# Preparing the next slab of a chunked recurrence over four steps instead of two, with masks on ScalarE and GpSimd and all scalings on GpSimd

## The chip, the cores and the metric

The kernel runs on one core of one Trainium2 chip. The metric is the device time of one execution in microseconds (us); lower is better. TensorE (PE in the rows; its weight loads are PEld), VectorE (DVE), ScalarE (ACT), GpSimd (POOL) and SyncE (SP, which here only issues DMAs) each run their own instruction stream in program order; they meet through semaphores.

## What is computed

Three stages in a row: a linear recurrence with a state of 40 x 40 for each of 32 (batch, head) pairs over 768 positions, a mixture-of-experts layer with one expert per token, and a dense feed-forward layer with squared ReLU. The change touches the first alone:

```python
for t in range(S):                               # S = 768, D = 40, B*H = 32
    kt, vt, rt = (k[:, :, t], v[:, :, t], r[:, :, t])
    wt, at, bt = (w[:, :, t], a[:, :, t], b[:, :, t])
    y[:, :, t] = np.einsum('bhd,bhde->bhe', rt, state)
    Sa = np.einsum('bhde,bhe->bhd', state, at)
    state_decay = state * wt[:, :, None, :] - np.einsum('bhd,bhe->bhde', Sa, bt)
    state = state_decay + np.einsum('bhd,bhe->bhde', vt, kt)
...
x = _moe_ref(x=x, **moe_kwargs)
return _moe2_ref(x=x, **moe2_kwargs)
```

## The kernel before

**Tiling.** The 768 positions are cut into 24 chunks of 32. Inside a chunk the recurrence becomes matrix products over all 32 heads, and one chunk is one step of the loop in `run` (c = 0 to 23). Four chunks are a slab; r = c % 4 is a step's place in its slab.

**One step** is a list of stages in the order of ORD: Z0 Z1 (the state against the chunk's operands, L214), Y0 Y1 (output of the chunk before, L259, brought to the tile xt by VectorE in steps r=0 and 1, and by ScalarE and GpSimd in r=2 and 3), U0 U1 (Ust, L231, which reads the inverse in tile tt), V0 V1, T0 T1 (transposes of the state, L250, copied to ys by ScalarE), K0 K1 (KBt, transposes of kb, L205, copied to ys by ScalarE), R (RUV, L141 with the tile ym, masked by VectorE at L143) and S0 S1 (Sst, the new state: L241 on TensorE, then tile m by VectorE at L244). Z0 of the next step waits for m. x_part (L405) brings finished outputs to the next stage of the network.

**Preparation of later slabs.** While a slab is worked on, the chunks of the slab after the next are prepared:
- `decay` (L108 to L112), once for each pair of chunks: four scans and two reciprocals on VectorE, from the loaded w; its last piece loads the w of a later pair.
- `prod` (L121, L124), once per chunk: a is scaled by pp, and the two halves of kb by qq. A string such as 'VGG' says which engine takes each of the three: V is VectorE, G is GpSimd.
- `L` (64 matmuls of `heads`, L141 with a, kb): the chunk's triangular matrix in PSUM, masked by VectorE into tile zs (L143), stored to DRAM (nt), loaded back in another layout (`tul`, tile tu), and `post`, two copies on ScalarE (L128, L129) and two small products on VectorE (dl).
- `inv` (L169 to L173): the inverse of all 128 triangular matrices of a slab in place in tu, 113 small operations on VectorE in one chain, then a store to DRAM (td); `ttfill` brings it from there into tile tt for Ust, a quarter per step.

**What sets the order.** The order is written out by hand. A step has 33 positions; stage k moves on by PW[k] of them (Z0 is position 0, Y0 2, U0 6, T1 14, K0 16, R 18, S0 20, S1 23), and what `sched` holds at a position is issued there, in program order on its engine. The tables, with d the step counted from the beginning of the slab two before the one that is prepared (so d=4 is the first step of the slab just before it):
- CA=(1, 2, 20): the first decay at d=1, over positions 2 to 20; CB=(3, 0, 20): the second at d=3, over 0 to 20.
- PA: for each of the four chunks d, position and engines of prod.
- LP: for each of the four chunks d and the stage behind which its L stands.
- IB=(0, 4, 6, 99): how much of the inverse (in estimated us) is issued in steps r=0 to 3; in r=1 from position 8 on, in r=3 over positions 0 to 14.

Slab 0 uses IB0 for the inverse of slab 1; chunks 0 to 7 are prepared ahead of the loop or in step 0. All loads and stores of this part are on SP's queue, in program order, among them kb (K1 of a step loads the chunk that stands 8 later) and the fill of tt.

In the rows, L141 with `a,kb` is L, with `r,ut` RUV.

## Time and profile before

| | us |
|---|---|
| median of three runs | 1075.1 (1071.02 to 1076.72) |
| the profiled execution | 1071.28 |
| its span, first to last instruction | 1069.5 |
| TensorE busy | 875.9 (82% of the span) |
| VectorE busy | 685.0 (64%) |
| ScalarE busy | 437.6 (41%) |
| GpSimd busy | 330.9 (31%) |

The shares are means over two very different parts: the recurrence up to about 530 us, and the feed-forward layers after it, where TensorE is nearly always busy. What a change in the recurrence is worth is read from its steps. A step here begins with the first matmul of Z0; step 4 begins at 149.2 us, step 20 at 460.9. "PEclk" in a table of stretches is TensorE's granted clock as a share of the full 2.4 GHz, so 0.50 is 1.2 GHz for the whole stretch. A wait is put down to what ended last before it; "issue" means that nothing in the profile shows what was waited for.

### The profile page before, as it was taken

The page shows a single profiled execution, that of the slowest core. Times are in us where ns is not written, and L with a number is a line of the kernel's source. Part 1 is how long each engine was busy: PE and PEld are TensorE (multiplying, and loading weights), DVE is VectorE, ACT ScalarE, POOL GpSimd, SP SyncE. Part 2 cuts the span into 40 slices and gives each one's busy share as a digit, 9 for nine tenths or more (in the row PEclk, how much of TensorE's full clock was granted, in tenths as well). Part 3 has the DMA queues.
Part 4 walks back from the last instruction along what each step waited for, and adds up shares of the span by engine and source line. Part 5 has one row for each costly group of instructions (what it writes and reads, how often), then busy time and mean ns, then how long its engine had stood idle before and what let it go on. Part 6 is the DMA issues. An engine that isn't in the chain of part 4 may idle for free.

```text
span 1069.5 us, 32862 instructions
## 1 busy us (share of the span) xinstructions
PE 875.9 (82%) x14040; PEld 836.1 (78%) x14040; DVE 685.0 (64%) x1621; ACT 437.6 (41%) x872; POOL 330.9 (31%) x292
## 2 busy tenths in 40 slices
PE   1137679888878877778769988889999999999996
PEld 1136668777767767767659888889999999999996
DVE  7997678867776878873559898555344444444331
ACT  6233245444434344445356445334333333344331
POOL 6032422611622526736443223261111111100000
PEclk9997576766766878897669999989999999999999
DMA  7547757457455547478469887711100111100000
GB/s 185 127 108 235 184 144 175 123 140 169 120 139 145 124 106 179 133 197 222 134 188 284 281 274 240 221 57 32 30 15 26 29 31 32 31 27 13 14 14 16
DMA packets 128144, 132.22 MB, mean 124 GB/s; under 512 B 80201, under 2 KB 104559, under 8 KB 127987
## 3 DMA queue, kind: packets, MB, share of 16 engines
q1 hardware_dynamic: 123731, 118.95, 41.0%
q0 software_dynamic: 4256, 11.06, 3.4%
q8 instruction: 112, 1.84, 0.7%
q14 instruction: 45, 0.37, 0.1%
HBM read 104.79 MB, written 29.70 MB: 126 GB/s over the span
## 4 chain that ended last, share of the span: by engine, by line
PE 56%; DVE 22%; DMA 10%; issue 6%; ACT 2%; POOL 1%; SPq 0%; DVEq 0%; POOLq 0%; ACTq 0%
PE fps L554 20%; PE fps L561 17%; PE pr L141 4%; PE ps L231 3%; PE pr L259 3%; DVE tu L170 2%; DVE m L244 2%; DVE tmp L169 2%; PE ps L220 2%; DVE qq L108 2%; PE ps L405 2%; DVE ym L143 2%; PE ps L250 2%; DVE zs L143 1%; PE ps L241 1%
## 5 line engine op out<-in xcount | busy, mean ns | idle before, releaser
L554 PE MATMUL fps<-xl,w1h 128*128 128x256 f32 x768 | 198.8, 286 | 12.7 <-DVE xl L544 12.7
L554 PE MATMUL fps<-xh,w1h 128*128 128x256 f32 x768 | 199.7, 287 | 2.8 <-ACT xh L543 2.2
L554 PEld LDWEIGHTS fps<-xl,w1h 128*128 128x128 f32 x768 | 149.0, 194 | 14.7 <-DVE xl L544 14.6
L561 PE MATMUL fps<-w2h,hh 128*128 128x320 f32 x512 | 158.7, 310 | 0.0
L561 PE MATMUL fps<-w2h,hl 128*128 128x320 f32 x512 | 158.2, 309 | 0.0
L561 PE MATMUL fps<-w2l,hh 128*128 128x320 f32 x512 | 158.2, 309 | 0.0
L554 PEld LDWEIGHTS fps<-xh,w1h 128*128 128x128 f32 x768 | 148.7, 194 | 4.1 <-ACT xh L543 3.1
L662 DVE TENSOR_TENSOR g<-r 128x512 f32<-128x512 f32 x96 | 68.2, 711 | 81.1 <-ACT r L661 81.1
L664 DVE TENSOR_TENSOR hl<-g,hh 128x512 fp32r<-128x512 f32 x96 | 76.0, 792 | 66.0 <-ACT hh L663 66.0
L554 PE MATMUL fps<-xh,w1l 128*128 128x256 f32 x512 | 103.9, 285 | 0.0
L663 ACT CAST hh<-g 128x512 fp32r<-128x512 f32 x96 | 59.6, 621 | 94.8 <-DVE g L662 94.8
L561 PEld LDWEIGHTS fps<-w2l,hh 128*128 128x128 f32 x512 | 96.1, 188 | 0.0
L561 PEld LDWEIGHTS fps<-w2h,hh 128*128 128x128 f32 x512 | 96.1, 188 | 0.0
L561 PEld LDWEIGHTS fps<-w2h,hl 128*128 128x128 f32 x512 | 96.1, 188 | 0.0
L124 POOL TENSOR_TENSOR kb<-kb,qq 104x512 f32<-104x512 f32 x48 | 63.9, 1354 | 87.2 <-DVE qq L108 25.8
L661 ACT ACTIVATE r<-fps 128x512 f32<-128x512 f32 x96 | 57.1, 594 | 76.6 <-PE fps L554 76.6
L141 PE MATMUL pr<-a,kb 40*64 40x32 f32 x1536 | 39.6, 265 | 51.9 <-POOL kb L124 29.3
L554 PEld LDWEIGHTS fps<-xh,w1l 128*128 128x128 f32 x512 | 80.4, 194 | 0.0
L141 PEld LDWEIGHTS pr<-a,kb 40*64 40x64 f32 x1536 | 36.7, 188 | 54.2 <-POOL kb L124 29.5
L170 DVE TENSOR_TENSOR tu<-tu,tmp 128x120 f32<-128x120 f32 (+25 forms) x312 | 76.7, 287 | 0.1
L259 PE MATMUL pr<-ym,ys 128*40 128x32 f32 x1536 | 49.6, 227 | 32.6 <-DVE xt L262 14.2
L169 DVE TENSOR_TENSOR tmp<-tu 128x120 f32<-128x120 f32 (+25 forms) x312 | 73.1, 272 | 0.5
(142 smaller groups left out, 1709.7 us busy)
## 6 DMA issues: line engine op xcount, KB each, us to landing
kb<-in_kb SPq DMA_DIRECT2D x24, 416.0 KB
ut<-in_vE SPq DMA_DIRECT2D x24, 416.0 KB
raw<-in_w SPq DMA_DIRECT2D x16, 512.0 KB
raw<-in_w SPq DMA_DIRECT2D x16, 480.0 KB
w<-in_w SPq DMA_DIRECT2D x12, 468.0 KB
a<-in_a SPq DMA_DIRECT2D x24, 208.0 KB
r<-in_r SPq DMA_DIRECT2D x24, 208.0 KB
c<-in_w_out SPq DMA_DIRECT2D x7, 640.0 KB
```

The costliest lines, as they stand in the source:

```text
L124: e[1+j].tensor_tensor(out=kv,in0=kv,in1=q[:,:,:,1:17],op=ALU.mult)
L141: nc.tensor.matmul(pt[64*hf:64*hf+64,r,32*p:32*p+32],w[k,8*hf+p,:],x[k,8*hf+p,:],start=True,stop=True)
L143: nc.vector.tensor_tensor(out=out[64:128,16*hf:16*hf+16].rearrange('p (x r) t -> p x r t',r=2), in0=pt[64*hf:64*hf+64,:,0:256].rearrange(' ...
L169: if k==0: V.tensor_tensor(out=tv,in0=Tv[:,j:j+1,b0:b0+n].to_broadcast([128,j,n]),in1=Tv[:,0:j,j:j+1].to_broadcast([128,j,n]),op=ALU.mult)
L170: else: V.tensor_tensor(out=w,in0=w,in1=tv,op=ALU.add)
L259: nc.tensor.matmul(pt[64*par:64*par+40,32*(k//2):32*(k//2)+32],ys[:,h,:],ym[:,h,:],start=True,stop=True)
L554: nc.tensor.matmul(pt[:,256*u:256*u+256],a,b,start=i==0,stop=i==len(ops)-1)
L561: nc.tensor.matmul(pt[:,0:320],a,b,start=first and n==0,stop=last and n==23); n+=1
L661: nc.scalar.activation(out=r,in_=v,func=AF.Relu)
L662: V.tensor_tensor(out=g,in0=r,in1=r,op=ALU.mult)
L663: nc.scalar.copy(out=gh[:,2*m2:2*m2+2],in_=g)
L664: V.tensor_tensor(out=gl[:,2*m2:2*m2+2],in0=g,in1=gh[:,2*m2:2*m2+2],op=ALU.subtract)
```

## The change

For all slabs but the first two:
- the first decay moves from d=1 (positions 2 to 20) to d=0 (positions 5 to 15); the second stays at d=3, over positions 0 to 8;
- prod of the four chunks goes to d=1, 2, 3 and 4 (before: 2, 2, 3 and 4), all three scalings on GpSimd;
- L stands behind S1 of d=1, 2 and 3, and behind T1 of d=4 (before: U1 and S1 of d=3, U1 and T1 of d=4);
- of the inverse, 8 instead of 4 estimated us are issued in r=1.

Chunks 8 to 11 (P == 2) have tables of their own, nearer to the old ones. For every chunk from 8 on, the mask of L is replaced: ScalarE copies from PSUM to zs with a factor of +1 or -1 per partition (the new tile sgn), and GpSimd sets the triangle above to zero with two affine_select instructions of 32 x 1024.

```diff
-    IB=(0, 4, 6, 99)
+    IB=(0, 8, 6, 99)
...
-    CA=(1, 2, 20)
-    PA=((2, 11, 'VGG'), (2, 12, 'GGG'), (3, 21, 'VGG'), (4, 2, 'VGG'))
-    CB=(3, 0, 20)
+    CA=(0, 5, 15)
+    CA2=(1, 2, 20)
+    PA=((1, 4, 'GGG'), (2, 2, 'GGG'), (3, 9, 'GGG'), (4, 0, 'GGG'))
...
+    CB=(3, 0, 8)
...
-    LP=((3, 'U1'), (3, 'S1'), (4, 'U1'), (4, 'T1'))
+    LP=((1, 'S1'), (2, 'S1'), (3, 'S1'), (4, 'T1'))
...
+        s.sgn=T('sgn',[128,1]); G.memset(s.sgn,1.0); G.memset(s.sgn[96:128],-1.0)
...
-    def heads(s,w,x,out,mask):
+    def heads(s,w,x,out,mask,later=False):
...
+        if later:
+            for hf in range(2):
+                nc.scalar.activation(out=out[64:128,16*hf:16*hf+16].rearrange('p (x r) t -> p x r t',r=2),
+                    in_=pt[64*hf:64*hf+64,:,0:256].rearrange('p r (x t) -> p x r t',t=32),func=AF.Copy,scale=s.sgn[64:128])
+            for b in (96,64):
+                nc.gpsimd.affine_select(out=out[b:b+32],in_=out[b:b+32],pattern=[[0,32],[1,32]],compare_op=ALU.is_ge,fill=0.0,base=-1,channel_multiplier=-1)
+            return
...
-        s.heads(kb,a,zs,s.mask[64:128,0])
+        s.heads(kb,a,zs,s.mask[64:128,0],c>7)
```

What stands on VectorE at the end of step 11 (r=3 of slab 2), before: the end of the inverse (L169 to L171, tile tu), the mask of L at U1 (L143, zs) among it, the second decay (L108, L112), then ym and m.

```order
L169 TENSOR_TENSOR tmp<-tu 128x52
L143 TENSOR_TENSOR zs_109<-pr,mask 64x512 x2
L132 TENSOR_TENSOR dl_132<-pp_100,qq_105 40x16
L133 TENSOR_TENSOR dl_132<-pp_100,qq_105 40x16
L112 RECIPROCAL inv<-pp_102 104x32
L170 TENSOR_TENSOR tu<-tu,tmp 128x26x3
L170 TENSOR_TENSOR tu<-tu,tmp 128x26x2
L169 TENSOR_TENSOR tmp<-tu 128x54 x2
L170 TENSOR_TENSOR tu<-tu,tmp 128x27x2 x2
L171 SCALAR_TENSOR_TENSOR tu<-tu 128x28 x3
L171 SCALAR_TENSOR_TENSOR tu<-tu 128x29
L108 SCALAR_TENSOR_TENSOR pp_102<-w_86,inv 104x576
```

The same place after (lines of the changed kernel: L112 and L116 are the decay, L180 to L182 the inverse):

```order
L116 RECIPROCAL inv<-pp_102 104x32
L181 TENSOR_TENSOR tu<-tu,tmp 128x25x3
L180 TENSOR_TENSOR tmp<-tu 128x78
L112 SCALAR_TENSOR_TENSOR pp_102<-w_86,inv 104x576
L180 TENSOR_TENSOR tmp<-tu 128x52
L112 SCALAR_TENSOR_TENSOR qq_106<-w_86,inv 104x576
L181 TENSOR_TENSOR tu<-tu,tmp 128x26x3
L181 TENSOR_TENSOR tu<-tu,tmp 128x26x2
L180 TENSOR_TENSOR tmp<-tu 128x54 x2
L181 TENSOR_TENSOR tu<-tu,tmp 128x27x2 x2
L182 SCALAR_TENSOR_TENSOR tu<-tu 128x28 x3
L182 SCALAR_TENSOR_TENSOR tu<-tu 128x29 x2
```

The mask and its dl products are gone from here, the decay's last scan (qq) has come ahead of the inverse's last operations, and only 23 of the inverse's 113 instructions are left in this step, where 47 stood; r=1 now has 55 instead of 32, r=2 35 instead of 34.

GpSimd from step 9 (r=1) into step 10 (r=2), before: the scatters of the finished slab (L428), the copy of xr, both halves of xt, then kb and a of the two chunks that are prepared.

```order
L450 COPY gt_200<-xr_196 128x4
L428 DMA xs<-xr_196,slot 2048x388 x4
L409 COPY xr_196<-xr_196 128x64
L262 TENSOR_TENSOR xt<-xt,pp_103 104x256 x2
L124 TENSOR_TENSOR kb_91<-kb_91,qq_105 104x16x32 x2
L121 TENSOR_TENSOR a_88<-a_88,pp_101 104x512
L124 TENSOR_TENSOR kb_92<-kb_92,qq_105 104x16x32 x2
```

After, with the first select of zs_109 waiting for the landing of the three later scatters:

```order
L440 DMA xs<-xr_199,slot 2048x388
L125 TENSOR_TENSOR a_87<-a_87,pp_101 104x512
L128 TENSOR_TENSOR kb_91<-kb_91,qq_105 104x16x32 x2
L440 DMA xs<-xr_199,slot 2048x388 x3
L421 COPY xr_199<-xr_199 128x64
L151 AFFINE_SELECT zs_109<-zs_109 32x1024 x2
L273 TENSOR_TENSOR xt<-xt,pp_103 104x256
L125 TENSOR_TENSOR a_88<-a_88,pp_101 104x512
L128 TENSOR_TENSOR kb_92<-kb_92,qq_105 104x16x32 x2
L273 TENSOR_TENSOR xt<-xt,pp_103 104x256
```

The first chunk's scalings have come a step earlier, in among the scatters; the second chunk's stand between the two halves of xt; the selects are new.

SP's queue in step 11, before: the store of the inverse (td), then the loads of w, kb, r and ut, then the fill of tt.

```order
L183 DMA td<-tu 128x1024
L97 DMA w_86<-in_w 104x1152
L101 DMA kb_94<-in_kb 104x1024
L197 DMA r<-in_r 104x512
L197 DMA ut<-in_vE 104x1024
L190 DMA tt<-td 32x8x32 x4
```

After:

```order
L101 DMA w_86<-in_w 104x1152
L194 DMA td<-tu 128x1024
L105 DMA kb_94<-in_kb 104x1024
L208 DMA r<-in_r 104x512
L208 DMA ut<-in_vE 104x1024
L201 DMA tt<-td 32x8x32 x4
```

The load of w has come ahead of the store.

## Rows read from the trace of the kernel before

**Rows 1.** Table of stretches, steps 7 to 16 and 20; columns named in its first line.

```profile
core 0: us, PE busy (x) PEld busy (x) DVE busy (x) ACT busy (x) POOL busy (x), PEclk, DMA share, GB/s
205.00:226.60 21.60, 19.02 (x496) 17.20 (x496) 21.20 (x67) 9.34 (x23) 8.26 (x6) 0.68 0.42 112
226.60:252.50 25.90, 21.20 (x512) 19.55 (x505) 11.39 (x31) 10.18 (x24) 2.58 (x3) 0.60 0.63 153
252.50:269.60 17.10, 13.12 (x369) 11.79 (x368) 16.44 (x64) 6.17 (x16) 5.03 (x5) 0.80 0.87 203
269.60:286.80 17.20, 14.81 (x369) 13.48 (x368) 10.45 (x42) 7.56 (x19) 12.18 (x8) 0.70 0.49 114
286.80:307.10 20.30, 15.68 (x497) 14.16 (x496) 19.96 (x65) 10.24 (x24) 8.71 (x6) 0.82 0.38 102
307.10:333.10 26.00, 22.92 (x509) 20.97 (x504) 12.58 (x33) 9.52 (x22) 3.04 (x3) 0.50 0.72 170
333.10:352.20 19.10, 14.90 (x369) 13.64 (x368) 15.35 (x61) 6.39 (x16) 6.35 (x5) 0.71 0.54 137
352.20:366.70 14.50, 11.35 (x369) 9.80 (x368) 12.91 (x42) 7.78 (x20) 11.68 (x8) 1.00 0.57 140
366.70:388.00 21.30, 16.60 (x500) 15.01 (x502) 20.93 (x66) 9.93 (x23) 8.42 (x7) 0.77 0.29 77
388.00:411.90 23.90, 18.31 (x506) 16.83 (x504) 17.01 (x34) 10.20 (x23) 10.51 (x9) 0.64 0.57 134
460.90:474.20 13.30, 11.78 (x373) 10.40 (x372) 7.79 (x20) 7.94 (x20) 5.36 (x5) 1.00 0.72 193
```

**Rows 2.** Chain of waits, 300 to 316 us: start, length, what.

```profile
302.56 4.67 DMA td<-tu
...
307.30 6.90 DMA tt<-td
```

**Rows 3.** TensorE in order of time, step 8: start, length, instruction.

```profile
234.00 2.49 PE L231 MATMUL ps<-z,tt 64*32 64x40 f32 x64
```

**Rows 4.** Table of stretches, VectorE's instructions on tile tu alone, step 11.

```profile
286.80:307.10 20.30, 8.98 (x46) 0.82 0.38 102
```

**Rows 5.** Groups of instructions by shape: total busy us, mean ns of one, idle before.

```profile
L143 DVE TENSOR_TENSOR zs<-pr,mask 64x512 f32<-64x512 f32 x48 | 33.1, 689 | 26.5 <-PE pr L141 25.8
...
L121 DVE TENSOR_TENSOR a<-a,pp 104x512 f32<-104x512 f32 x18 | 15.5, 868 | 0.1
...
L121 POOL TENSOR_TENSOR a<-a,pp 104x512 f32<-104x512 f32 x6 | 8.0, 1328 | 14.1 <-DVE pp L108 14.1
...
L661 ACT ACTIVATE r<-fps 128x512 f32<-128x512 f32 x96 | 57.1, 594 | 76.6 <-PE fps L554 76.6
```

**Rows 6.** Line 108 (the decay's scans): durations in ns, min/median/max.

```profile
L108 DVE TENSOR_TENSOR_SCAN pp<-w,one x12: 1331/1350/2282, 7.0 to 371.7; 104x576 f32<-104x576 f32 x12
```

**Rows 7.** GpSimd in order of time, steps 10 and 17.

```profile
271.83 6.16 POOL L262 TENSOR_TENSOR xt<-xt,pp 104x256 f32<-104x256 f32 x2 [1.39 <-ACT xt L261]
...
421.14 1.59 POOL L727 TENSOR_TENSOR c64t<-c64t,c 128x640 int32<-128x640 int32 x1
```

**Rows 8.** VectorE in order of time, step 17, beside the second row above.

```profile
420.87 2.79 DVE L170 TENSOR_TENSOR tu<-tu,tmp 128x65 f32<-128x65 f32 x2
```

**Rows 9.** TensorE in order of time: L of one chunk in steps 11 and 12.

```profile
291.94 1.14 PE L141 MATMUL pr<-a,kb 40*64 40x32 f32 x64
...
316.92 1.93 PE L141 MATMUL pr<-a,kb 40*64 40x32 f32 x64
```

**Rows 10.** GpSimd's groups at the start: its selects, mean ns of one.

```profile
L70 POOL TENSOR_SCALAR_AFFINE_SELECT mask<-mask 32x64 f32<-32x64 f32 x2 | 0.5, 240 | 0.1
...
L379 POOL TENSOR_SCALAR_AFFINE_SELECT us<-us 128x128 f32<-128x128 f32 x1 | 0.3, 292 | 0.1
```

**Rows 11.** SP's queue in order of time: when the loads of kb were issued.

```profile
304.57 0.33 SPq L101 DMA_DIRECT2D kb<-in_kb  x1
...
330.30 0.49 SPq L101 DMA_DIRECT2D kb<-in_kb  x1
```

**Rows 12.** GpSimd in order of time, step 12: the scaling that waited for kb.

```profile
310.70 2.80 POOL L124 TENSOR_TENSOR kb<-kb,qq 104x512 f32<-104x512 f32 x2 [3.75 <-DMA kb<-in_kb]
```

More of the change, by code (lines that the diff above doesn't have):

```diff
@@ L28 @@
     F3=0
-    CA=(1, 2, 20)
-    PA=((2, 11, 'VGG'), (2, 12, 'GGG'), (3, 21, 'VGG'), (4, 2, 'VGG'))
-    CB=(3, 0, 20)
+    CA=(0, 5, 15)
+    CA2=(1, 2, 20)
+    PA=((1, 4, 'GGG'), (2, 2, 'GGG'), (3, 9, 'GGG'), (4, 0, 'GGG'))
+    PA2=((2, 2, 'GGG'), (2, 8, 'GGG'), (3, 9, 'GGG'), (4, 0, 'GGG'))
+    CB=(3, 0, 8)
     SC=(2, 14)
     L0=('R', 'S1')
-    LP=((3, 'U1'), (3, 'S1'), (4, 'U1'), (4, 'T1'))
+    LP=((1, 'S1'), (2, 'S1'), (3, 'S1'), (4, 'T1'))
+    LP2=((2, 'S1'), (3, 'U1'), (3, 'S1'), (4, 'T1'))
     YP=(0, 0, 1, 1)
@@ L312, in run @@
                 if P>=s.NS or P<2: continue
-                if d==4: at(0,*[lambda x=x: s.tul(x) for x,(e,st) in zip(range(2*A,2*A+4),s.LP) if e<4])
-                if d==s.CA[0]: add(s.decay(A),*s.CA[1:])
+                CA,PA,LP=(s.CA2,s.PA2,s.LP2) if P==2 else (s.CA,s.PA,s.LP)
+                if d==4: at(0,*[lambda x=x: s.tul(x) for x,(e,st) in zip(range(2*A,2*A+4),LP) if e<4])
+                if d==CA[0]: add(s.decay(A),*CA[1:])
                 for k in range(4):
-                    e,p,w=s.PA[k]
+                    e,p,w=PA[k]
                     if d==e: at(p,lambda x=2*A+k,w=w: s.prod(x,eng(w)))
-                    e,st=s.LP[k]
+                    e,st=LP[k]
                     if d==e: Ls.setdefault(st,[]).append(2*A+k)
```

## The prediction

> **What bounds the kernel now.** I read the table of stretches first, one row per step, then the chain of waits at a slab's border, then who holds which engine there. The feed-forward part (from 530 us on) is not touched, so everything is decided in the scan, steps 1 to 19. Its steps differ by position r in the slab. The last rows of the table hold the yardstick: step 20, with no preparation left, takes 13.3 us at a granted clock of 1.00 [rows 1]. Against it r=3 takes 21.6, 20.3 and 21.3, and VectorE is busy for 21.20, 19.96 and 20.93 of that: VectorE bounds r=3. r=1 is bounded by it as well (16.44 busy of 17.1; 15.35 of 19.1). r=0 takes 25.9, 26.0 and 23.9 with VectorE at only 11.39, 12.58 and 17.01: there TensorE is busy 21 to 23 us at clocks of 0.60 and 0.50, so the matmuls run mostly at the lower of the two levels (1.2 GHz) after a step in which TensorE had waited. r=2 is the cheapest, 17.2 at clock 0.70 and 14.5 at clock 1.00 [rows 1].
>
> Between r=3 and r=0 lies a chain: the last column of the inverse on VectorE, the store td (302.56, 4.67 us), the fill tt (307.30, 6.90 us), ending at 314.20 [rows 2], on which Ust of r=0 waits. From the start of r=3 (286.8) that is 27.4 us; one slab earlier Ust began at 234.00 [rows 3], 29.0 after 205.0. Mean 28.2. A shorter r=3 is worth only what this chain gives.
>
> **The change, part by part, for one full slab** (three of them: the pairs of steps 7-8, 11-12 and 15-16).
>
> (1) *From r=3 to Ust of r=0.* In r=3, 24 of the 47 operations of the inverse are gone (23 go to r=1, one to r=2). 46 of them took 8.98 us [rows 4], 0.195 each: -4.7. The mask of the chunk that stood at U1 goes from VectorE: two instructions of 0.689 [rows 5], -1.4, and it stood ahead of the inverse's end. The second decay is squeezed into positions 0 to 8, so its fourth scan, which stood behind the inverse, now stands ahead: +1.35 [rows 6]. The end of the inverse was 15.8 after the step's start (302.56 less 286.8 [rows 1, 2]), and comes to 11.0. But the three scalings of the third chunk are now on GpSimd in the same stretch, and they need the scans just ahead of the last columns. Two operations of the two engines that both read two SBUF operands don't run together: a GpSimd operation of 1.59 us beside a pair of inverse operations that lasted 2.79 [rows 7, 8] instead of the 0.4 that 0.195 each gives; and a pair of GpSimd operations of 256 elements that took 6.16 us under VectorE's back-to-back work [rows 7], where one of 512 takes 1.33 [rows 5]. So either VectorE stands for 3 x 1.33 = 4.0, and the inverse ends at 15.0, or GpSimd waits and it ends at 11.0. I take the middle, 13.0. From there to tt it was 11.65 (302.56 to 314.20 [rows 2]). The w load that stood between td and the fill now stands ahead of td; the fill can gain from nothing to the 2.2 that bring its 6.90 down to td's 4.67; I take 1. Ust starts at 13.0 + 10.65 = 23.6 instead of 28.2: **-4.6**, bounds -7.8 and -1.5. Late next is tt itself: r=3 ends earlier than it lands, so part of what VectorE is relieved of only lengthens the wait in r=0.
>
> (2) *From Ust of r=0 to r=1.* This took 18.5 (234.0 to 252.5) and 18.9 (314.2 to 333.1) [rows 1 to 3]. Two chunks' L stood in it, now one: -1.93 at the lower level [rows 9]. Its two masks run on ScalarE, ahead of the ys copies that Sst waits for: two of about 0.594, the nearest row for 512 elements from PSUM [rows 5], 0 to +1.2; TensorE has KBt and RUV between, which hide it at the lower clock. **-1.5**, bounds -1.9 and -0.7. The first decay, now here, takes 5.4 of VectorE's idle time. The nt store, which the tul, the next kb and ut loads stand behind on SP, waits for GpSimd's first select instead of VectorE's mask. Selects of 64 and 128 elements took 0.240 and 0.292 [rows 10], so 1024 take about 1.0 by that slope. Store and kb load go 1.2 later (0.59 x 2 and 1.0 against 1.4, rounded up for the handover).
>
> (3) *r=1.* VectorE loses four scans (5.4) and gains 23 operations of the inverse (4.5): 15.9 busy comes to 15.0. The scalings of the first chunk can stop it for up to 4.0. So 15 to 19 against lengths of 17.1 and 19.1: **0**, bounds -2 and +2. The kb load was issued at 304.57 [rows 11] and GpSimd got its data at 310.70 [rows 12], 6.1 later; the load for this step was issued at 330.30, so its data come at 336.4, or 337.6 with the delay of (2), 4.5 into r=1. Three scatters and the copy of xr are queued behind that wait on GpSimd, and the step's selects wait for the scatters to land, with the nt store behind them on SP; the loads that follow there (v, ra, tt, kb) have most of a step of slack.
>
> (4) *r=2.* A chunk's L now stands behind S1: 1.14 at the higher level, 1.93 at the lower [rows 9], part of it in the wait for m. Behind it on ScalarE stand z and the xt copies of the next step, up to 1.2 later each. **+1.2**, bounds -0.5 and +3. Scalings of a cost GpSimd 1.33 where VectorE took 0.868 [rows 5].
>
> The sgn memsets lie in GpSimd's idle start and cost nothing; without that cover they would be two memsets at the start.
>
> **The sum.** -4.6 - 1.5 + 0 + 1.2 = -4.9 a slab, -14.7 for three. Slab 0 is prepared by the old table with the new masks and scalings: half, -2.5. In slab 4 the inverse alone moves from step 19 to step 17: 4.5 us go over, between -4.5 and +4.5, taken as 0. Together -17. The profiled execution took 1071.3 (span 1069.5, 1.8 around it), so 1054; the median of the three runs is 1075.1, 3.8 above that execution, and I put the forecast on it: **1058**. Bounds by the terms: three slabs between -12.2 and +2.8 each, so 1075 less 37 and plus 8, with the ends 1031 to 1088.
>
> **The rivals.**
> *The clock stays up (B).* If r=3 no longer leaves TensorE waiting, r=0 runs at 2.4 GHz. The same L took 1.93 and 1.14 [rows 9], a ratio of 0.59; 18.7 us behind Ust come to 11.0, 7.7 less for each of three slabs, -23 on top: 1035. For it: step 14 at 1.00 took 14.5 [rows 1]. Against it: the wait for tt in r=0 stays, and grows.
> *Nothing is left (C).* VectorE stands still for all of GpSimd's scalings: (1) -1.5, (2) -0.7, (3) +2, (4) +1: 0.8 a slab, +2 in all, 1077. For it: the 2.79 us pair [rows 8].
> *GpSimd becomes the bound (D), slower.* In r=2 its queue is: half of xt, three scalings, the other half of xt, as the rows of the order show. If each group waits as the pair of [rows 7] does (6.16 less 1.33 for the same 512 elements: 4.8), it takes 6.16 + 4.8 + 4.0 = 15.0; it starts some 2.2 into the step (271.83 less 269.6), so x_part and L behind S1 get their data at 17.2, and with L and x_part the step ends at about 19.5 against 15.9: +3.6. TensorE waits for that, and the next step runs at the lower clock, 17.2 against 14.5 for a step of the same work [rows 1]: +2.7. With (1) -1.5, (2) -0.7 and (3) +2 that is +6.1 a slab, +18: 1094. It decides from the point where GpSimd's data for L come later than S1, some 13 us into the step. For it: the 6.16; against it: VectorE has less to do in r=2 (10.45 and 12.91 busy [rows 1]), so GpSimd should wait in one group, not two.
>
> The Trainium skill speaks against this change: "GPSIMD Engine Reference", section "Engine selection", gives elementwise work with two inputs to VectorE, as GpSimd takes about twice as long, and its "Key points" say that it shares SBUF interfaces with VectorE and collides with VectorE instructions that read two SBUF operands. The trace agrees with both (1.33 against 0.868, and the 2.79 us pair). By that rule alone the time would be that of C or D.
>
> **Chances.** A (forecast) 0.48; B 0.19; C 0.16; D 0.17. About 0.5% (5 us) is what a measurement of this kernel can tell from no change. Faster: A and B, 0.67. Same: C, 0.16. Slower: D, 0.17. The range leaves out the lower third of B and the upper part of D: 1031 to 1086.
>
> **What would show it.** r=3 at 16 to 19 us with VectorE still busiest; td issued 11 to 15 us into r=3 and Ust of r=0 some 23.6 after r=3's start; r=0 at 20 to 24; r=1 within 2 of 18; r=2 one longer. L behind S1 should not wait for kb. Wrong would be: r=2 or r=1 at 19 and more with TensorE waiting for kb or xt (D); pairs of inverse operations over 2 us in all steps (C); r=0 at a clock near 1.00 (B).

## The result, and the profile after

The changed kernel is slower: 1085.1 us (median) against 1073.5 us of the kernel before on the same chip, a ratio of 1.0121 (95% interval 1.0077 to 1.0165). On a second chip it was 1083.9 against 1073.3, 1.0094 (1.0058 to 1.0129). So it costs 10 to 13 us, where a gain of 17 was forecast. The 1085.1 us still lie inside the stated range (1031 to 1086), at its slow end; the direction was wrong. The profile taken with the first times fell on a disturbed execution (1925 us, with TensorE's matmuls at about twice their usual time), so the profile after is that of the run e1_after below, an execution of 1083.6 us.

> The changed kernel as it is, for a profile of an undisturbed execution. Expected 1.012 of the kernel before, some 1087 us, since that is what its times gave. By the forecast's own steps r=3 should be 16 to 19 us long, Ust of r=0 come 23.6 us after the start of r=3, r=0 take 20 to 24, r=1 17 to 19, r=2 one more than before. Theory D (GpSimd is the bound): r=2 or r=1 at 19 us and more, TensorE waiting there for what GpSimd makes. Theory C (VectorE stands still for GpSimd): pairs of operations of the inverse over 2 us in all four steps and r=3 no shorter than 20. Theory M (the masks on ScalarE and GpSimd): waits of TensorE for z and xt copies, 1 to 3 us in each step with an L behind S1. The step that is longer than before names the one to follow.

The table of stretches of the changed kernel, in the columns of [rows 1]: steps 3, 5 to 17, and last the whole scan from step 0 to the end of step 22.

```profile
133.10:154.60 21.50, 16.88 (x500) 15.31 (x496) 21.25 (x43) 12.42 (x27) 11.85 (x10) 0.76 0.39 100
...
177.30:196.00 18.70, 17.55 (x435) 16.11 (x434) 16.84 (x78) 6.80 (x17) 8.49 (x9) 0.59 0.73 183
196.00:212.60 16.60, 14.75 (x436) 13.17 (x432) 16.32 (x45) 9.93 (x23) 8.01 (x8) 0.79 0.49 123
212.60:232.90 20.30, 15.48 (x440) 13.88 (x432) 19.96 (x40) 9.93 (x23) 11.63 (x8) 0.77 0.36 97
232.90:254.70 21.80, 15.27 (x440) 13.72 (x436) 12.04 (x28) 12.13 (x26) 8.77 (x8) 0.75 0.74 177
254.70:276.00 21.30, 16.76 (x433) 15.05 (x432) 19.07 (x86) 6.58 (x17) 9.92 (x9) 0.73 0.67 169
276.00:295.20 19.20, 17.56 (x440) 16.09 (x438) 13.05 (x45) 9.92 (x23) 11.08 (x8) 0.59 0.43 109
295.20:311.90 16.70, 14.02 (x436) 12.79 (x432) 16.53 (x33) 9.82 (x23) 9.63 (x8) 0.80 0.41 105
311.90:334.10 22.20, 19.29 (x443) 17.30 (x436) 14.05 (x30) 12.12 (x26) 9.84 (x8) 0.58 0.82 176
334.10:354.60 20.50, 18.54 (x438) 17.09 (x440) 17.55 (x80) 6.80 (x17) 7.92 (x9) 0.54 0.58 154
354.60:370.30 15.70, 11.97 (x437) 10.60 (x436) 15.49 (x43) 9.71 (x23) 8.00 (x8) 1.00 0.48 121
370.30:389.90 19.60, 18.28 (x432) 16.62 (x432) 19.29 (x39) 10.03 (x23) 10.04 (x8) 0.57 0.21 54
389.90:412.80 22.90, 17.74 (x444) 15.90 (x437) 8.30 (x27) 12.91 (x27) 12.92 (x11) 0.74 0.68 155
412.80:436.40 23.60, 13.38 (x369) 12.17 (x368) 21.66 (x80) 7.50 (x18) 16.45 (x16) 0.72 0.61 180
48.20:520.20 472.00, 364.66 (x9696) 329.98 (x9696) 362.23 (x1069) 213.34 (x496) 225.06 (x193) 0.72 0.60 153
```

The same view of the kernel before: the whole scan, and steps 3, 5, 6 and 17, which [rows 1] does not show.

```profile
48.20:509.00 460.80, 356.18 (x9698) 323.23 (x9700) 347.04 (x1114) 192.54 (x464) 186.94 (x149) 0.75 0.61 157
133.00:149.20 16.20, 14.07 (x497) 12.95 (x496) 15.87 (x46) 10.24 (x24) 4.22 (x6) 0.89 0.41 108
172.30:189.90 17.60, 16.04 (x371) 14.79 (x370) 16.66 (x63) 6.22 (x16) 6.45 (x5) 0.60 0.81 194
189.90:205.00 15.10, 13.52 (x371) 12.31 (x370) 10.38 (x40) 7.90 (x20) 11.43 (x8) 0.75 0.44 108
411.90:430.80 18.90, 12.55 (x371) 11.32 (x372) 16.89 (x60) 7.39 (x18) 12.21 (x12) 0.86 0.73 175
```

The scan takes 472.0 instead of 460.8, which is nearly all of the difference between the two executions. r=3 and r=0 (steps 7, 8, 11, 12, 15, 16) are 123.5 us instead of 139.0 in sum, as they should be. But r=1 (steps 5, 9, 13) takes 60.5 instead of 53.8, step 3 takes 21.5 instead of 16.2, and step 17 takes 23.6 instead of 18.9. And VectorE, which lost 32 masks of 0.689 and twelve scalings of 0.868 [rows 5], is busy for 362.2 us instead of 347.0. Something else made its work longer.

How far does one execution differ from the next? The kernel before was run once more for a second profile.

> The kernel before once more, for a second profile of it: how far the steps of one kernel differ between executions. Its first profile was of 1071.3 us, 4 below the median of its three runs. Expected 1073 to 1082, the same order of steps, single steps up to 3 us longer or shorter where TensorE's granted clock differs, and TensorE's idle time in steps 0 to 22 between 100 and 108 us.

It took 1082.1 us. Its table: the whole scan, step 3, step 17.

```profile
48.00:519.20 471.20, 377.69 (x9696) 343.50 (x9696) 349.92 (x1113) 192.69 (x464) 186.00 (x149) 0.70 0.60 153
133.60:151.00 17.40, 15.86 (x497) 14.68 (x496) 17.10 (x48) 10.24 (x24) 5.59 (x6) 0.77 0.44 118
420.00:437.90 17.90, 13.86 (x371) 12.43 (x370) 16.37 (x60) 7.26 (x18) 10.12 (x10) 0.81 0.70 185
```

With the same instructions TensorE is busy for 377.7 us instead of 356.2, at a mean granted clock of 0.70 instead of 0.75, and idle for 93.5 instead of 104.6. A single profile's sum therefore says little about 10 us. Steps 3 and 17 differ by only 1.2 and 1.0 between the two, so their 4 to 6 us in the changed kernel stand out. The three slabs between (steps 5 to 16) are shorter in the changed kernel than in both: 235.5 us against 239.6 and 242.3. VectorE's busy time differs by less between the two executions (347.0 and 349.9), and it is the safer thing to compare.

The part behind the scan, from the start of step 23 to the end, differs too, though its code is the same: 560.5 and 561.1 us in these two, 561.5 in the changed kernel, and 551.9 to 561.5 over all kernels below. So an execution's time is not its scan's alone. What a part is worth is read from the ratios below; a profile shows how, and does not always show where.

### The profile page after: what moved, and what is told of

The parts are those of the page before. It is cut to its first block, busy times and chain, and to the rows that moved or that the text cites. A ratio compares the mean times of both kernels' runs of the same rounds, so it can differ in the third digit from the quotient of the medians.

```text
span 1923.2 us, 32930 instructions
## 1 busy us (share of the span) xinstructions
PE 1817.6 (95%) x14040; PEld 1706.4 (89%) x14040; DVE 678.4 (35%) x1577; ACT 469.8 (24%) x904; POOL 355.4 (18%) x338
## 4 chain that ended last, share of the span: by engine, by line
PE 90%; DVE 4%; issue 2%; ACT 1%; DMA 1%; POOL 1%; SPq 0%; POOLq 0%; DVEq 0%
PE fps L566 32%; PE fps L573 30%; PE pr L145 5%; PE ps L252 4%; PE ps L242 4%; PE ps L417 3%; PE ps L231 3%; PE ps L261 3%; PE pr L270 3%; PE ps L216 2%; PE fps L553 2%; DVE qq L112 1%; PE ps L225 1%; POOL kb L128 1%; DMA a<-in_a 0%
## 5 line engine op out<-in xcount | busy, mean ns | idle before, releaser
L566 PE MATMUL fps<-xh,w1h 128*128 128x256 f32 x768 | 406.0, 533 | 1.8 <-ACT xh L555 1.1
L566 PE MATMUL fps<-xl,w1h 128*128 128x256 f32 x768 | 404.3, 530 | 0.3
L566 PEld LDWEIGHTS fps<-xh,w1h 128*128 128x128 f32 x768 | 332.8, 433 | 4.9 <-ACT xh L555 2.4
L566 PEld LDWEIGHTS fps<-xl,w1h 128*128 128x128 f32 x768 | 333.8, 435 | 1.7 <-DVE xl L556 1.2
L573 PE MATMUL fps<-w2h,hh 128*128 128x320 f32 x512 | 310.8, 607 | 0.0
L573 PE MATMUL fps<-w2h,hl 128*128 128x320 f32 x512 | 310.6, 607 | 0.0
L573 PE MATMUL fps<-w2l,hh 128*128 128x320 f32 x512 | 309.8, 605 | 0.0
L566 PE MATMUL fps<-xh,w1l 128*128 128x256 f32 x512 | 211.8, 529 | 0.0
L573 PEld LDWEIGHTS fps<-w2l,hh 128*128 128x128 f32 x512 | 186.4, 364 | 13.6
L566 PEld LDWEIGHTS fps<-xh,w1l 128*128 128x128 f32 x512 | 189.0, 439 | 0.0
L180 DVE TENSOR_TENSOR tmp<-tu 128x120 f32<-128x120 f32 (+25 forms) x312 | 93.1, 336 | 0.5
```

The costliest lines, as they stand in the source:

```text
L180: if k==0: V.tensor_tensor(out=tv,in0=Tv[:,j:j+1,b0:b0+n].to_broadcast([128,j,n]),in1=Tv[:,0:j,j:j+1].to_broadcast([128,j,n]),op=ALU.mult)
L566: nc.tensor.matmul(pt[:,256*u:256*u+256],a,b,start=i==0,stop=i==len(ops)-1)
L573: nc.tensor.matmul(pt[:,0:320],a,b,start=first and n==0,stop=last and n==23); n+=1
```

## VectorE's inverse, the same work at another price

VectorE's instructions on the tile tu (the inverse, 480 of them) from 130 to 470 us, stretch and busy time: the kernel before, whole and in step 9.

```profile
130.00:470.00 340.00, 97.74 (x480) 0.73 0.58 144
...
252.50:269.60 17.10, 4.71 (x32) 0.80 0.87 203
```

The changed kernel; then the same tile in its steps 9, 11 and 15.

```profile
130.00:470.00 340.00, 136.60 (x480) 0.70 0.56 140
...
254.70:276.00 21.30, 11.18 (x57) 0.73 0.67 169
295.20:311.90 16.70, 9.71 (x22) 0.80 0.41 105
...
370.30:389.90 19.60, 7.30 (x22) 0.57 0.21 54
```

The same 480 operations cost 39 us more. In step 11, r=3, 46 of them took 8.98 [rows 4]; now the 22 that are left take 9.71, and 7.30 in step 15. The forecast's largest gain, 24 operations out of r=3, is not there in VectorE's time on tu. The instructions of that step show why: VectorE and GpSimd in order of time.

```profile
304.20 1.34 DVE L181 TENSOR_TENSOR tu<-tu,tmp 128x78 f32<-128x78 f32 x2
305.47 2.39 DVE L180 TENSOR_TENSOR tmp<-tu 128x54 f32<-128x54 f32 x2
307.78 0.33 DVE L181 TENSOR_TENSOR tu<-tu,tmp 128x54 f32<-128x54 f32 x2
...
302.99 2.48 POOL L125 TENSOR_TENSOR a<-a,pp 104x512 f32<-104x512 f32 x1 [1.45 <-DVE pp L112]
305.44 2.35 POOL L128 TENSOR_TENSOR kb<-kb,qq 104x512 f32<-104x512 f32 x2
```

A pair of a kind that takes 0.33 alone (the next row) takes 2.39, and ends at 307.86, with GpSimd's two scalings of kb (307.79); the pair before it lasts 1.34 and ends with the scaling of a. VectorE stands still for GpSimd's whole instruction. GpSimd is held as well: its scaling of a takes 2.48 here, where 1.328 was the mean before [rows 5], and began beside a scan of VectorE (302.93 to 304.28). The forecast had asked which of the two waits; here both do. GpSimd's new selects do the same, though they have one input only; step 3 of the changed kernel, VectorE and then GpSimd:

```profile
135.00 2.40 DVE L112 TENSOR_TENSOR_SCAN pp<-w,one 104x576 f32<-104x576 f32 x1
137.32 1.44 DVE L180 TENSOR_TENSOR tmp<-tu 128x92 f32<-128x92 f32 x2
...
134.70 3.96 POOL L151 TENSOR_SCALAR_AFFINE_SELECT zs<-zs 32x1024 f32<-32x1024 f32 x2 [1.88 <-ACT zs L148]
```

A scan of 1.35 [rows 6] takes 2.40, and a pair of the inverse 1.44, beside selects that last until 138.66. The Trainium skill, "GPSIMD Engine Reference", section "Key points", says that GpSimd shares its SBUF interfaces with VectorE and collides with VectorE instructions that have two SBUF inputs; the trace agrees, and prices it at the whole length of GpSimd's instruction.

## Experiments: one part undone, one part alone

All ratios below are to runs of the kernel before on the same chip; 0.001 is 1.1 us.

**Masks back on VectorE** (of the 16 chunks of slabs 2 to 5; the 24 in the expectation counts two slabs whose masks were never moved).

```diff
-        s.heads(kb,a,zs,s.mask[64:128,0],c>7)
+        s.heads(kb,a,zs,s.mask[64:128,0])
```

> The changed kernel with the masks of all chunks on VectorE as before; everything else as changed. In the changed kernel each L gives ScalarE two instructions of 0.69 us and GpSimd two selects of 1.3 us, 24 times; beside the selects a pair of VectorE's inverse operations takes 1.4 us instead of 0.4, and Z0 and the xt copies stand behind ScalarE's two. Theory M (the masks cost the gain): VectorE takes back 1.4 us a chunk but loses the stalls, TensorE's waits for xt and for L shrink: 10 to 16 us below the changed kernel, 0.995 to 1.00 of before. Theory Q (VectorE's in-order queue: the inverse columns moved into r=1 stand ahead of the copies m that Z0 waits for): VectorE gets longer by 1.4 us in every step: the same as the changed kernel or up to 6 slower, 1.008 to 1.018 of before.

Measured 1.0036 (0.9997 to 1.0075), 6 to 9 us below the changed kernel: between the two theories. So the masks are part of the loss in this company, less than M had it; with intervals of 0.004 to either side, the 6 to 9 us are known to some 6.

**The inverse's columns divided as before**, in the changed kernel, and **that part alone**, in the kernel before.

```diff
-    IB=(0, 8, 6, 99)
+    IB=(0, 4, 6, 99)
```

> The changed kernel with the inverse's columns divided as before (four columns a position in r=1 instead of eight). In the changed kernel's trace step 17 has TensorE waiting 7.76 us for m behind some 27 inverse operations on VectorE, 3.60 before. Theory Q: r=1 gets shorter by 3 to 5 us in each of steps 5, 9, 13 and 17, r=3 longer by 4 again: step 17 alone brings 4 to 5 net, as it has no r=3 with scans behind it; in all 0.998 to 1.008 of before, 2 to 12 us below the changed kernel. Theory M: r=3 gets 4.5 us longer in three steps with nothing given back: 8 to 14 us above the changed kernel, 1.017 to 1.022 of before.

> The kernel before with one part of the change: eight columns of the inverse a position in r=1. The decay scans of r=1 stay there (5.4 us) and 23 inverse operations come (4.5 us), so VectorE in r=1 has 20 to 21 us of work where the step took 17.1 to 19.1; r=3 loses 4.5. Theory Q: r=1 grows by 3 to 5, r=3 and the chain td, tt behind it shrink by 4 to 5: within 0.5% of before, 0.996 to 1.005, with step 17 longer by 3 to 4. Theory M says the inverse's move is a gain that the masks eat: 0.985 to 0.992 of before.

Undoing it did not help: 1.0164 (1.0093 to 1.0234, only four runs), which cannot be told from the changed kernel but lies above Q's 0.998 to 1.008. Theory Q, that the columns moved into r=1 are the loss, falls. In its profile r=1 is no shorter with four columns (20.6 us on average, 20.2 in the changed kernel). In its step 9, the row below, VectorE is busy for 13.6 only, but TensorE for 18.1:

```profile
260.60:280.70 20.10, 18.13 (x433) 16.44 (x432) 13.61 (x60) 6.59 (x17) 7.99 (x9) 0.61 0.74 176
```

Alone, in the kernel before, the inverse's move gave 1.0044 (1.0004 to 1.0083), as Q expected where the scans stay in r=1 too. The table of that run, steps 9 and 11:

```profile
256.80:276.80 20.00, 14.02 (x370) 12.13 (x369) 19.44 (x84) 6.71 (x17) 5.95 (x6) 0.76 0.72 170
292.50:308.60 16.10, 13.74 (x500) 12.00 (x504) 15.78 (x41) 9.44 (x23) 5.08 (x6) 1.00 0.44 123
```

VectorE's time on tu in its step 11:

```profile
292.50:308.60 16.10, 4.61 (x22) 1.00 0.44 123
```

With nothing new on GpSimd the 22 operations take 4.61 and r=3 is 16.1 us instead of 20.3: this is the gain that the forecast had worked out. r=1 takes 20.0 with VectorE busy for 19.4, and gives most of it back.

**The masks alone**, in the kernel before (the edit is that of the diff's function heads, with c>7).

> The kernel before with one part of the change: the masks of the chunks from the third slab on by ScalarE and GpSimd. Theory M: slower than before by 6 us or more, 1.006 to 1.015. Theory Q and the forecast's step: VectorE loses 24 x 1.38 us, of which that in r=3 counts: 3 to 8 us faster than before, 0.993 to 0.998.

Measured 1.0043 (0.9997 to 1.009). It does not show the gain that the forecast's side expected; whether it costs anything, the interval leaves open.

**Spreading alone, and two halves of the way there.** The first kernel keeps from the change only the tables for decays and inverse; the second has L in its new places as well; the third has L in its old places but the scalings of a on GpSimd. In all three the masks are on VectorE, and the tables of slab 0 (PA2, LP2) are changed in the same way as those shown.

```diff
-    PA=((1, 4, 'GGG'), (2, 2, 'GGG'), (3, 9, 'GGG'), (4, 0, 'GGG'))
+    PA=((1, 4, 'VGG'), (2, 2, 'VGG'), (3, 9, 'VGG'), (4, 0, 'VGG'))
-    LP=((1, 'S1'), (2, 'S1'), (3, 'S1'), (4, 'T1'))
+    LP=((3, 'U1'), (3, 'S1'), (4, 'U1'), (4, 'T1'))
```

> The changed kernel with masks and scalings of a back on VectorE and every L where it stood before: of the change only the spreading of decays and inverse over the four steps is left. By the runs so far the masks cost some 6 us of the changed kernel's 10 to 13, and the inverse's move alone takes 4.3 off each r=3 but gives it back in r=1, where the decay's scans still stood (5.4 us) in the same queue. Theory S (spreading is sound; GpSimd, ScalarE and L's new place took its gain): r=1 no longer holds both, so r=3 is 3 to 4 us shorter than before and r=1 at most 1 longer: 0.985 to 0.995. Theory L (TensorE's lower clock returns whatever is saved: its idle time comes to 95 to 108 us in the scan in every kernel so far, and what varies is its busy time): 0.998 to 1.005, with idle time of TensorE as before and its busy time 8 to 15 us more.

> The changed kernel with masks and scalings of a back on VectorE; L stays behind S1 in r=1 to r=3. Against the kernel with the masks alone back (1.0036 of before) it prices the scalings on GpSimd. If each of GpSimd's scalings stands still VectorE or is stood still by it (1.2 to 2.4 us each in the trace, where VectorE takes 0.87): 4 to 8 us better, 0.996 to 1.000. If GpSimd's scalings lie beside VectorE's work: 0 to 3 us worse, 1.003 to 1.007.

> The changed kernel with the masks back on VectorE and every L where it stood before; scalings of a stay on GpSimd. Against the kernel with the masks alone back (1.0036 of before) it prices the new places of L. If L behind S1 costs TensorE 1.1 to 1.9 us a step between S and Z that the wait for m does not hide (r=2: 17.2 and 14.5 before, 19.2 and 15.7 changed): 3 to 8 us better, 0.996 to 1.001. If the forecast's step holds (in r=0 two L cost 1.5 a slab more than one): 0 to 4 us worse, 1.003 to 1.008.

Measured 1.0081 (1.0046 to 1.0116), 1.0023 (0.9986 to 1.0059) and 1.0093 (1.0053 to 1.0132). Two things follow. L behind S1 is worth 6 us (1.0081 to 1.0023; 1.0093 to 1.0036), more than either branch of the third expectation gave; and the spread without it loses, against theory S and, by its middle value, beyond theory L. A wait that goes with it can be seen in step 3 of the first kernel (TensorE, VectorE and GpSimd in order of time) and again in its step 11, an r=3 (the last two rows, TensorE and VectorE).

```profile
147.82 1.93 PE L145 MATMUL pr<-r,ut 40*64 40x32 f32 x64 [6.16 <-issue]
...
142.68 2.36 DVE L180 TENSOR_TENSOR tmp<-tu 128x78 f32<-128x78 f32 x2
...
146.33 1.39 DVE L154 TENSOR_TENSOR zs<-pr,mask 64x512 f32<-64x512 f32 x2
...
142.61 2.36 POOL L128 TENSOR_TENSOR kb<-kb,qq 104x512 f32<-104x512 f32 x2 [4.40 <-PE ps L216]
...
307.82 1.93 PE L145 MATMUL pr<-r,ut 40*64 40x32 f32 x64 [3.86 <-issue]
...
306.33 1.39 DVE L154 TENSOR_TENSOR zs<-pr,mask 64x512 f32<-64x512 f32 x2
```

RUV writes the PSUM tile pr that L at U1 has filled, and must wait for its mask; the mask ends at 147.72, RUV starts at 147.82 (the row itself names no releaser). The mask now stands on VectorE behind all four scans and a pair held by GpSimd for 2.36; TensorE waits 6.16 us, and 3.86 in step 11. In r=3 of the second kernel, which has its L behind S1 there, RUV waits for no mask; what follows L there is Y of the next step, which also writes pr and waits for the mask 1.2 us at the longest (7.3 in eight times). In step 3 the second kernel keeps one L at U1, and RUV waits 3.56 there as well. So these waits are of the right kind and size for the 6 us, but that they make up the whole of it is not shown.

## Experiments: where the loss sits

**The old tables at the two ends of the scan**: for the slab prepared in steps 0 to 4 (its scans, scalings and L), and for the last slab's inverse in step 17. The first kernel is the changed one with both, the second with the first alone; the third has both, and masks and scalings of a on VectorE.

```diff
-    PA2=((2, 2, 'GGG'), (2, 8, 'GGG'), (3, 9, 'GGG'), (4, 0, 'GGG'))
-    LP2=((2, 'S1'), (3, 'U1'), (3, 'S1'), (4, 'T1'))
+    PA2=((2, 11, 'VGG'), (2, 12, 'GGG'), (3, 21, 'VGG'), (4, 2, 'VGG'))
+    CB2=(3, 0, 20)
+    LP2=((3, 'U1'), (3, 'S1'), (4, 'U1'), (4, 'T1'))
...
-                ib=s.IB if sl else s.IB0
+                ib=(s.IB if n2 else (0, 4, 6, 99)) if sl else s.IB0
```

> The changed kernel with the old tables at its two ends alone: the slab that is prepared in steps 0 to 4 has its scans, scalings and L where they stood before (its masks stay on ScalarE and GpSimd), and the last slab has four columns of the inverse a position in step 17 again. In the changed kernel steps 0 to 3 take 106.4 us against 101.0 and 103.0 in two profiles of before, nearly all of it in step 3 (21.6 against 16.2 and 17.4), and step 17 takes 23.6 against 18.9 and 17.9. Theory E (the loss sits at the ends, where the spread buys nothing since no r=3 behind it gets shorter): 7 to 10 us below the changed kernel, 1.001 to 1.004 of before. Theory L (TensorE's lower clock returns what is saved): step 3 and step 17 get shorter and others longer, 1.008 to 1.013.

> The changed kernel with the old tables for the slab prepared in steps 0 to 4 alone. Theory E: step 3 goes from 21.6 to 17 or 18 us, 3 to 6 us below the changed kernel, 1.004 to 1.008 of before; step 17 stays at 22.5 to 24. Theory L: step 3 gets shorter, but steps 4 to 6 get longer by as much, 1.009 to 1.013.

> Decays and inverse spread and L behind S1 as in the changed kernel for the three slabs between, with masks and scalings of a on VectorE as before, and the old tables at both ends. The same with the new tables at the ends took 1.0023 of before, with step 3 at 24.8 (16.2 and 17.4 before) and step 17 at 23.5 (18.9 and 17.9). Theory E: 7 to 11 us of that go, 0.992 to 0.996 of before, faster than both kernels. Theory L: TensorE's clock returns it, 0.998 to 1.004.

Measured 1.0008 (0.9976 to 1.004), 1.0035 (0.9994 to 1.0077) and 0.9952 (0.9914 to 0.9991). Theory E's ranges agree with all three intervals, theory L's lie outside the first two: the ends are worth 8 us (1.0023 to 0.9952) to 12 (1.0121 to 1.0008). The larger part seems to be at the first slab (1.0035 with its old tables alone), though the two intervals overlap. In the third kernel (medians 1067.3 us against 1076.0) the two steps are back to what they were; steps 3 and 17 of its table:

```profile
133.20:149.80 16.60, 15.43 (x501) 14.17 (x501) 15.70 (x46) 9.65 (x23) 5.57 (x6) 0.78 0.38 98
412.80:431.20 18.40, 14.96 (x371) 13.58 (x372) 14.81 (x58) 7.04 (x17) 9.16 (x8) 0.70 0.44 124
```

In the first two the profile of step 3 stays at 21.4 and 20.6, with VectorE's work down from 21.2 to 16.9 and 17.0 but TensorE at a clock of 0.58 and 0.67; in which step their time was gained the single profiles don't tell. In the first, the scan as a whole takes 471.2 where the changed kernel's took 472.0; of the 7.7 us between the two profiled executions 6.4 lie behind the scan. So that the ends' tables cost 8 to 12 us is shown by the times; how they do so at the first slab stays open. Step 17 shows its cause more plainly. The changed kernel there, TensorE, VectorE and GpSimd:

```profile
436.44 0.28 PE L225 MATMUL ps<-m,zs 128*32 128x40 f32 x2 [7.76 <-DVE m L255]
...
422.04 2.44 DVE L180 TENSOR_TENSOR tmp<-tu 128x78 f32<-128x78 f32 x2
...
435.90 1.00 DVE L255 TENSOR_TENSOR m<-ps,dl 40x320 f32<-40x320 f32 x2
...
422.72 1.59 POOL L739 TENSOR_TENSOR c64t<-c64t,c 128x640 int32<-128x640 int32 x1
```

The copies m, on which Z of the next step waits, stand on VectorE behind 23 inverse operations more than before (55 against 32 in the step), and pairs of them are held to 1.8 and 2.4 us by GpSimd's preparation for the feed-forward part, as a pair was before [rows 8]. Before, that wait was 3.60. And there is no busy r=3 behind it for which this would pay: step 19 takes 15.6, against 14.2 and 16.9 in the two profiles of the kernel before. A step 17 with the old columns can be as long for another reason: it took 23.0 in the profile of the fastest kernel below, with TensorE at a granted clock of 0.50 (1.2 GHz) all through it.

**Which move to GpSimd costs.** Four kernels on the third one of above (0.9952): GpSimd's selects on top, ScalarE's copies on top, masks moved wholly, and six columns of the inverse in r=1 instead of eight. Then the scalings of a moved alone, and, in the changed kernel itself, the scalings alone undone (the last change below the other way round, for slab 0 as well). The edits, cut to what differs:

```diff
+        if later:
+            for b in (96,64):
+                nc.gpsimd.affine_select(out=out[b:b+32],in_=out[b:b+32],...)
...
+        if later:
+            for hf in range(2):
+                nc.scalar.activation(out=out[64:128,16*hf:16*hf+16]...,func=AF.Copy,scale=s.sgn[64:128])
...
-        s.heads(kb,a,zs,s.mask[64:128,0])
+        s.heads(kb,a,zs,s.mask[64:128,0],c>7)
...
-    IB=(0, 8, 6, 99)
+    IB=(0, 6, 6, 99)
...
-    PA=((1, 4, 'VGG'), (2, 2, 'VGG'), (3, 9, 'VGG'), (4, 0, 'VGG'))
+    PA=((1, 4, 'GGG'), (2, 2, 'GGG'), (3, 9, 'GGG'), (4, 0, 'GGG'))
```

> The kernel with the old tables at both ends and masks and scalings of a on VectorE (0.9952 of before), and GpSimd's two selects run on top in each of the 16 L, on data that VectorE has masked already (they change nothing). Theory G (the selects on GpSimd are what the masks cost, by holding up VectorE's operations with two SBUF inputs and by delaying the nt store): 4 to 7 us above 0.9952: 0.999 to 1.002, pairs of the inverse of 1.4 us beside them. Theory A (ScalarE's copies are the cost): 0.994 to 0.998.

> The same kernel (0.9952 of before) with ScalarE's two copies run on top in each of the 16 L, ahead of VectorE's masks, which write the same tile after them. Theory A: ScalarE gets 1.4 us more ahead of z, xt and the ys copies, and the mask comes 0.7 to 1.4 later: 4 to 8 us above, 0.999 to 1.003. Theory G: 0.994 to 0.998.

> The same kernel (0.9952 of before) with the masks of the 16 L moved to ScalarE and GpSimd as in the change; scalings of a stay on VectorE. With those on GpSimd too it was 1.0008. If the masks make that difference: 0.998 to 1.003. If the scalings make it: 0.994 to 0.998.

> The same kernel (0.9952 of before) with six columns' worth of the inverse in r=1 instead of eight. r=1 takes 19.9 us on average in it against 18.4 and 17.9 in two profiles of before. If the inverse's share in VectorE's queue there is the rest: r=1 one shorter, r=3 one longer, with the chain td, tt behind it: 0.994 to 0.999. If r=1 stays as long, the cause is L behind its S1 (1.1 to 1.9 us on TensorE), and r=3 alone pays: 0.997 to 1.001.

> Old tables at both ends, masks on VectorE, scalings of a of the three slabs between on GpSimd. Theory P (a scaling on GpSimd costs by itself, being 1.3 us or more where VectorE takes 0.87, ahead of L): 6 us above the kernel with it on VectorE (0.9952): 0.999 to 1.003. Theory I (only masks and scalings together fill GpSimd's queue so far that TensorE's L or VectorE waits): 0.993 to 0.998.

> The changed kernel with the scalings of a back on VectorE, masks on ScalarE and GpSimd, the new tables at the ends. Theories P and I both: 5 to 9 us below the changed kernel (1.0094 and 1.0121 of before), 1.001 to 1.006. If the scalings cost nothing and the kernel with masks moved alone was fast for another reason: 1.008 to 1.013.

On top, both cost: selects 1.0079 (1.0053 to 1.0106), copies 1.0052 (1.0017 to 1.0088), 14 and 11 us above the kernel without them, more than either theory gave. But moved wholly the masks cost nothing: 0.9936 (0.9904 to 0.9968), the fastest of all, 1075.0 against 1081.6 us. So theories G and A, by which a part of the move is the cost, both fall. That the two runs price an instruction more in the chain from L to the nt store, and not the move, is the likely reading, but argued. Six columns are no better than eight, 0.9987 (0.9953 to 1.0021): in its profile r=1 stays as long (20.4 us in steps 5, 9 and 13, against 20.5) and r=3 grows from 18.1 to 20.3. The scalings moved alone cost nothing either, 0.9969 (0.994 to 0.9998), and undone in the changed kernel they bring 1.0017 (0.9986 to 1.0048). Two squares result:

| masks / scalings of a | both on VectorE | masks moved | scalings moved | both moved |
|---|---|---|---|---|
| old tables at the ends | 0.9952 | 0.9936 | 0.9969 | 1.0008 |
| new tables at the ends | 1.0023 | 1.0017 | 1.0036 | 1.0094, 1.0121 |

In both rows either move alone is within 2 us of none, and both together cost 6 to 11: theory I, against P. Each ratio's interval is some 0.0035 to either side, so one such difference alone would be weak; that two rows show it is what the reading rests on. What the pair costs beyond the sum of the two moves is 6 us in the first row and 8 in the second, each known to some 7 by these intervals; and the ratios of a row come from several chips, each to the kernel before on its own. VectorE's time on tu from 130 to 470 us grows with each move (97.74 in the kernel before). Old tables, neither moved:

```profile
130.00:470.00 340.00, 113.76 (x480) 0.70 0.56 143
```

The same with the masks moved:

```profile
130.00:470.00 340.00, 124.08 (x480) 0.69 0.56 140
```

With the scalings moved alone it is 120.1, with both 130.5. By the times the first 10 us of it cost nothing and the next do; that this is VectorE's slack being used up is argued, not shown. One pair of rows speaks for it, TensorE's waits for m from 130 to 470 us (us in total, times, longest). Old tables, both moved:

```profile
PE ps L226 <- DVE m L256: 6.3, 10, 3.6
```

The fastest one (old tables, masks moved):

```profile
PE ps L226 <- DVE m L256: 1.6, 7, 0.3
```

With neither moved it is 1.4, with the scalings alone 1.7. But the 3.6 stand at the end of step 17, and in the second row of the table these waits follow no such order: 11.9 with neither moved, 2.1 with the masks, 8.3 with the scalings, 11.5 with both, most of it at the end of step 17 again. Where in the scan the two moves together cost their time stays open.

## Why the prediction was wrong

Per full slab, in the two profiles (steps 5 to 16, three slabs):

| step of the prediction | forecast | measured |
|---|---|---|
| (1) from r=3 to Ust of r=0 | -4.6 (-7.8 to -1.5) | -2.3 (26.3 against 28.6) |
| (2) from Ust to r=1 | -1.5 (-1.9 to -0.7) | -2.9 (14.8 against 17.8) |
| (3) r=1 | 0 (-2 to +2) | +2.2 (20.2 against 17.9) |
| (4) r=2 | +1.2 (-0.5 to +3) | +1.6 (17.2 against 15.6) |
| steps 3 and 17, at the ends | part of -2.5, and 0 (-4.5 to +4.5) | +5.3 and +4.7 |

In sum that is -1.4 a slab where -4.9 were forecast; against the second profile of the kernel before it is -2.3. So the three slabs gained, but less than half as much, and the ends lost.

**(1)** got the place right and half of the size wrong. The inverse ended 16.9, 14.2 and 17.1 us into r=3, on average 16.1 and not 13.0; before it was 16.6, 15.8 and 16.7, on average 16.4, so it hardly moved. The forecast had weighed the chunk's three scalings (a and both halves of kb) at 4.0 and taken half; they held the last pairs for 3.1 in each of the three steps (in step 11, 1.34 and 2.39 where 0.33 is usual). It had not counted what GpSimd runs ahead of them in the same step, the selects and the products xt: beside those a scan took 2.30 in step 15, and pairs 1.43 in steps 7 and 11. What came off is the rest of the chain, 10.3 us from the inverse's end to Ust instead of 12.2 (28.6 less 16.4; forecast 10.65). The chain of waits between steps 11 and 12 (4.67 and 6.90 in [rows 2]):

```profile
309.37 3.18 DMA td<-tu
...
313.44 5.35 DMA tt<-td
```

**(2)** was larger than its bound: one L less, and less of r=0 at the lower clock (0.75, 0.58 and 0.74 against 0.60, 0.50 and 0.64). Together (1) and (2) are -5.2 against -6.1.

**(3)** failed. A slab has four L. Before, two stood in r=3 and two in r=0; now there is one in each step. The forecast took one out of r=0 and put one into r=2, but the one that left r=3 and the one that came into r=1 stand nowhere in its sum. It weighed r=1 by VectorE's time alone, which was to fall from 15.9 to 15.0; it rose from 16.2 to 17.8, as the 23 operations that came were priced at 0.195, 4.5 in all, and VectorE spent 6.5 and 6.7 more on tu in steps 9 and 13 (11.18 and 11.43 against 4.71 and 4.73). But what fills the longer step is TensorE: over steps 5, 9 and 13 it is busy for 17.6 us instead of 14.7, at a mean clock of 0.62 instead of 0.70, and idle for 2.5 instead of 3.2. L (1.14 or 1.93 [rows 9]) is the work that came. The profiles of two runs separate the causes: with only four columns of the inverse in r=1 the step still took 20.6 on average, with VectorE busy for 14.3; with eight columns but every L in its old place (the first kernel of the spreading) it took 18.4, and 19.4 with the scalings of a on GpSimd besides (the third). Why the clock is lower there is not shown.

**(4)** was right.

**The sum** failed most at the ends. Slab 0 was given "half" of the gain, -2.5, by analogy and without a look at step 3, where GpSimd's selects now run beside the scans (the scan of 2.40 above) and which took 4 to 5 us more. Slab 4's shift into step 17 was called 0 with the row for its price already on the page: the held pair of 2.79 [rows 8] and the GpSimd instruction beside it [rows 7] stand in step 17 itself. Undoing the ends gave back 8 to 12 us. With the ends as before and one or both of the two moves to GpSimd left out, the change gains 3 to 7 us of the 14.7 that were forecast for the three slabs.

**The rivals.** The time lay between C (1077) and D (1094). D's place was wrong: r=2 is 1.6 longer, not 3.6, and TensorE waits there for nothing of GpSimd's. C's mechanism, VectorE standing still for GpSimd, is there in r=3; C priced it by the scalings alone and at the three full slabs alone, and so stopped at no change. No rival had the ends, nor L in r=1. The slower side had 0.17, little for a change that kept GpSimd busy for 225.1 - 186.9 = 38 us more, an engine that VectorE waits for.

## What to carry to other kernels

Before work goes to GpSimd, list what VectorE runs beside it: in these traces an instruction of VectorE with two SBUF inputs can cost its own time plus the whole of GpSimd's instruction, and a move that hides alone may not hide with a second one. When work moves between steps, book it at both places, and for every engine: what leaves one step arrives in another (here L in r=1). A table that shifts work earlier pays only where the step that gets shorter was the bound; at the first and the last turn of a pipeline look up that step by itself, and keep the old table where nothing behind it gets shorter. Undo the parts singly and in pairs: here the change became 0.3 to 0.6% faster than the kernel before by leaving out its two ends and one or both of the moves to GpSimd.

## What was not expected of the hardware

- A select of GpSimd on 32 partitions with one input held VectorE's two-input instructions on 128 partitions as a two-input scaling did (a pair of 0.4 took 1.44 beside it). The selects were held too: half of the 32 took 1.26 us or less, the longest 4.72. VectorE's copies m, which read PSUM and SBUF, kept their mean of 488 ns, before and after.
- Two executions of one kernel, with the same instructions, put TensorE's scan at 356.2 busy and 104.6 idle, and at 377.7 busy and 93.5 idle: less idle time went with a lower mean clock (0.70 against 0.75), and with 10.4 us more in sum.
